# An attention and maxout kernel: weight loads cut in halves and moved among the first value casts, w_out asked for ahead of a cast, and two small swaps of order

## The chip, the cores and the metric

One core of a Trainium2 chip runs the whole program. The metric is the device time of one execution in microseconds (us). Three executions of the kernel before took 290.01 to 290.74 us, median 290.72.

## The reference

Attention over 8 batches and 8 heads, with 576 queries of width 64, whose keys and values are 16 beacon rows followed by 576 causal rows; the result, turned to 4608 tokens of width 512, goes through a feed-forward layer that takes the maximum of three products before the last one.

```python
B, H, S, Nb, D = (8, 8, 576, 16, 64)
k_all = np.concatenate([beacon_k, k], axis=2)
v_all = np.concatenate([beacon_v, v], axis=2)
scores = scale * np.matmul(q, k_all.transpose(0, 1, 3, 2))
scores = np.where(causal, -1000000000.0, scores)      # causal part only for the 576 rows
a = np.exp(scores - scores.max(-1, keepdims=True))
a /= a.sum(-1, keepdims=True) + 1e-09
x = np.matmul(a, v_all).transpose(0, 2, 1, 3).reshape(B * S, H * D)
h = np.maximum(np.maximum(x @ w1, x @ w2), x @ w3)     # w1..w3: 512 x 768
return h @ w_out                                       # w_out: 768 x 512
```

All inputs and the output are float32 in HBM.

## The kernel before

The work goes by pairs of heads: 4 pairs to a batch (`PPB`), 32 in all, two pairs to a quad. For a pair, PE turns q and k so that the width lies on the partitions (L410 for batch 0, L391 later; from batch 4 on, transposing DMAs do it), then computes the scores by tiles of 128 keys. ACT takes the exponential into `at_sb`. GpSimd (POOL) sets the causal part of the diagonal tiles to zero (`affine_select`, L538) or, where `dve` is given, VectorE (DVE) multiplies it with a triangle (L536). PE then multiplies with ones (the sums) and with the values `v_sb` (L582 in batch 0, L615 later), ACT inverts the sums by Ln and Exp, and DVE multiplies (L661 in batch 0, L638 later) into `xT`, the input of the feed-forward layer. That layer runs as units of eight or four matmuls (L720 for the first tokens, L691 later, L739 for the last product with `w_out`), which are slotted in between the attention steps, so that PE always has something to do.

The order is written out by hand; there is no scheduler. Every engine works through its own list in the order of the program, and so do the two issuers of loads: SP (hardware queue q1), which loads q, k, v and the beacons as float32 and stores the output, and POOL (software queue q0), whose DMAs cast to bfloat16 on the way: the quads of q and k for batch 0 (L253), the three input weights (L329, one DMA for each half of 256 rows) and `w_out` (L334). A DMA that POOL issues therefore waits until POOL has done what stands ahead of it.

The steps that the change touches stand in `first_batch` and `second_batch`, in short names. `T` turns a half pair and `S_(p, g)` computes the scores of group g of pair p and their exponential (L483 and L492). `M(p, g)` masks a group; with `True` it does so on DVE, else on POOL. `V(t)` casts value tile t of batch 0 on POOL (L319), after its load on SP has landed. `P(quad, half)` multiplies with ones and values. `invert_sums` and `multiply` make the products L661: for each quad and half three of them, kept in a list from which `multiply(count)` takes the first. `F()` emits the next unit of the feed-forward layer; its first six are the products of the first 256 tokens with weight 1 (three units) and weight 2 (three), each a pair of 128 columns, eight matmuls; the matmuls of a unit read all four row tiles of the weight, that is both halves.

In `second_batch` the masks of a pair of batch 1 alternate with casts on POOL: `cast_piece` and `cast_pair` (L262) for the q and k of pairs further on, `cast_v` (L307) for the values of batch 1. `next_load` takes the next load of batches 2 and on from a list and issues it on SP; the buffers that the loads go to are eight in turn, and a load waits until the cast that read the buffer before has been made. The beacons of batches 4 to 7 come in that same list ahead of the loads of batch 4; POOL casts them at L813.

Of the kernel before, what the change touches and what calls it, by code (L numbers as in the profile page):

```python
# [16 lines left out]
def kernel(  # L17
# [13 lines left out]
    nc = tc.nc  # L31
# [5 lines left out]
    d_model, d_ff = moe_w1.shape  # L37
# [21 lines left out]
    n_quad = 2  # L59
# [108 lines left out]
    w_in = [const.tile([128, n_ct, d_ff], BF16, name=f"w{i}_sb") for i in range(3)]  # L168
# [48 lines left out]
    def load_pair(p, gate=None):  # L217
        b, g, j0 = place(p)
        hs = slice(head(g, j0), head(g, j0) + 2)
        st = new_stage(("pair", p))  # L220
        if gate:
            gate.memset(st[0:QP, 0:1], 0.0)
        for i, src in enumerate((q, k)):
            nc.sync.dma_start(
                out=st[0:QP, i * NQ2 : (i + 1) * NQ2].rearrange("p (h x) -> p h x", h=2),
                in_=src[b, hs].rearrange("h (p r) d -> p h (r d)", r=QR),
            )
# [47 lines left out]
    def load_v(b, piece, gate=None):  # L275
        st = new_stage(("v", b, piece))
        if gate:
            gate.memset(st[:, 0:1], 0.0)
        t_lo, t_hi = V_PIECES[piece]
        for t in range(t_lo, t_hi):  # L280
            i = t - t_lo
            dst = st[:, i * H * D : (i + 1) * H * D].rearrange("p (h d) -> p h d", h=H)
            lo = 0
            if t == 0:
                lo = Nb
                nc.sync.dma_start(
                    out=dst[0:Nb], in_=beacon_v[b].rearrange("h n d -> n h d")
                )
            t0 = k_tok[t] + lo
            n = k_rows[t] - lo  # L290
            nc.sync.dma_start(
                out=dst[lo : lo + n], in_=v[b, :, t0 : t0 + n, :].rearrange("h p d -> p h d")
            )

    def cast_v(b, piece, cast):
        st = stage.pop(("v", b, piece))
        if b not in v_tiles:
            v_tiles[b] = v_pool.tile([128, n_kt, H, D], BF16, name="v_sb")
        v_sb = v_tiles[b]
        t_lo, t_hi = V_PIECES[piece]  # L300
        t = t_lo
        while t < t_hi:
            t1 = t + 1
            while t1 < t_hi and k_rows[t1] == k_rows[t]:
                t1 += 1
            n = k_rows[t]
            cast(  # L307
                v_sb[0:n, t:t1].rearrange("p t h d -> p (t h d)"),
                st[0:n, (t - t_lo) * H * D : (t1 - t_lo) * H * D],
            )  # L310
            t = t1
# [11 lines left out]
        if t + 1 == V_PIECES[piece][1]:  # L323
            stage.pop(("v", 0, piece))

    def load_w(i, f0, f1):
        wv = (moe_w1, moe_w2, moe_w3)[i].rearrange("(g p e) f -> g p e f", g=n_quad, e=2)
        for g in range(n_quad):
            nc.gpsimd.dma_start(  # L329
                out=w_in[i][:, 2 * g : 2 * g + 2, f0:f1], in_=wv[g, :, :, f0:f1]  # L330
            )

    def load_w_out():
        nc.gpsimd.dma_start(  # L334
            out=w_out_sb, in_=moe_w_out.rearrange("(t p) m -> p t m", p=128)
        )
# [60 lines left out]
    def fill(at_bank, n):  # L397
        for _ in range(n):
            nc.tensor.matmul(
                acc[:, at_bank], busy[:, 0:128], busy, start=True, stop=True  # L400
            )
# [242 lines left out]
    def invert_sums():  # L644
        if not unfinished:
            return
        quad, hf = unfinished.pop(0)
        ps = pv_tiles.pop((quad, hf))
        recip = nrm_pool.tile([128, S], FP32, name="recip")[:, 0:HALF]
        nc.scalar.activation(out=recip, in_=ps[0][:, 0:HALF], func=AF.Ln)  # L650
        nc.scalar.activation(out=recip, in_=recip, func=AF.Exp, scale=-1.0)
        for n in range(1, len(passes)):
            products.append((quad, hf, n, ps, recip))

    def multiply(count=len(passes)):
        for _ in range(min(count, len(products))):
            quad, hf, n, ps, recip = products.pop(0)
            b, g = divmod(quad, n_quad)
            c0 = b % RING * S + hf * HALF
            part, bank, lo, ca, cb = passes[n]  # L660
            nc.vector.tensor_mul(  # L661
                xT[:, 2 * g + part - 1, c0 + ca : c0 + cb],
                ps[bank][:, lo : lo + cb - ca],
                recip[:, ca:cb],
            )
            if g == n_quad - 1 and n == len(passes) - 1:
                ready[0] = 2 * b + hf
# [129 lines left out]
    def emit_ffn(limit, new_ps=ffn_psum.tile, close=False):  # L797
        if not may_emit(limit):
            return False
        need, fn, args = units[done[0]]  # L800
        done[0] += 1
        fn(*args, new_ps, *([True] if close else []))
        return True
# [23 lines left out]
    def next_load(n=1):  # L827
        for _ in range(n):
            if loads:
                loads.pop(0)()  # L830
# [45 lines left out]
    S_, T, M, P, V = emit_scores, turn_part, emit_masks, emit_pv, cast_first_v  # L876

    def F(n=1, new_ps=ffn_psum.tile):
        for _ in range(n):
            assert emit_ffn(END, new_ps)  # L880

    def first_batch():
        S_(0, 0)
        T(2, 0, 0, 6)
        S_(1, 0)
        T(2, 0, 1, 7, None, 3)
        T(3, 0, 0, 4)
        T(3, 0, 1, 5)
        V(0)
        V(1)  # L890
        fill(6, 2)
        S_(2, 0)
        M(0, 0, True)
        T(0, 1, 0, 6)
        T(1, 1, 0, 4)
        S_(3, 0)
        M(1, 0, True)
        T(0, 1, 1, 7, None, 2)
        T(1, 1, 1, 5)
        V(2)  # L900
        load_w(0, 0, d_ff)
        S_(0, 1)
        T(2, 1, 0, 6)
        S_(0, 2)
        M(2, 0, True)
        M(0, 1)
        S_(0, 3)
        T(2, 1, 1, 7, None, 2)
        T(3, 1, 0, 6)
        S_(1, 1)  # L910
        M(3, 0, True)
        T(3, 1, 1, 7)
        V(3)
        M(0, 2)
        V(4)
        P(0, 0, 0, 1)
        S_(1, 2)
        M(0, 3, True)
        P(0, 0, 1)
        M(1, 1)  # L920
        invert_sums()
        S_(1, 3)
        P(1, 0, apart=True)
        M(1, 2)
        invert_sums()
        M(1, 3, True)
        load_w(1, 0, d_ff)
        multiply()
        S_(2, 1)
        by_pool(bk16_1, bk32_1)  # L930
        multiply()
        load_pair(PPB, nc.vector)
        for p in range(PPB + 1, 2 * PPB):
            load_pair(p)
        load_v(1, 0)
        load_v(1, 1)
        next_load(2)
        S_(2, 2)
        P(0, 1)
        S_(2, 3)  # L940
        M(2, 1)
        invert_sums()
        F()
        S_(3, 1)
        M(2, 2)
        multiply()
        F()
        S_(3, 2)
        M(2, 3, True)
        F()  # L950
        S_(3, 3)
        M(3, 1)
        M(3, 2)
        M(3, 3, True)
        cast_pair(PPB, by_pool, by_pool)
        next_load()
        P(1, 1)
        invert_sums()
        turn_beacons(1, B_PE, bk16_1)
        F(2)  # L960
        turn_pair(PPB, by_act)
        place_beacons(PPB, by_act)
        cast_pair(PPB + 1, by_pool, by_pool)
        next_load()
        load_w(2, 0, d_ff)
        F()
        multiply()
        free_banks[:] = [2, 3, 0, 1, 6, 7, 4, 5]

    def second_batch():  # L970
        for p in range(PPB, 2 * PPB):
            place_beacons(p + 1, by_act)
            emit_burst(p)
            for gi in range(NG):
                emit_masks(p, gi)
                if p < PPB + 2 and 0 < gi < 3:
                    cast_piece(p + 2, gi - 1, by_pool)
                if p == 2 * PPB - 1 and gi == 1:
                    cast_v(1, 1, by_pool)
                    next_load()  # L980
            if p < PPB + 2:
                stage.pop(("pair", p + 2))
                next_load()
            if p == PPB + 2:
                cast_v(1, 0, by_pool)
                next_load()
                load_w_out()
            if p + 1 < 2 * PPB:
                turn_pair(p + 1, by_dve)
                F(2, next_psum)  # L990
        F(4, next_psum)
        for p in range(2 * PPB, 2 * PPB + 2):
            cast_pair(p, by_pool, by_pool)
            next_load()
        finish = emit_pv_whole(n_quad)
        turn_pair(2 * PPB, by_dve)
        F(2, next_psum)
        finish()
# [94 lines left out]
```

## Time and profile before

| | |
|---|---|
| Runs | 290.01, 290.72, 290.74 us |
| The profiled execution | 289.66 us, span 287.9 us, clock 1.00 |
| PE busy | 276.0 us, 96% of the span |
| DVE, ACT, POOL busy | 173.8, 159.8, 135.7 us |
| DMA | 50.59 MB moved, mean 176 GB/s |
| Chain that ended last, by engine | PE 79%, DMA 12%, POOL 3%, ACT 2%, DVE 1% |
| DMA in that chain | w_out 4%, v 4%, w1 to w3 3%, q 1% |
| Weight 1 to 3, per half | 384 KB, median 7.6 us from issue to landing |
| w_out | 768 KB, 12.4 us from issue to landing |

The span is counted from the program's first instruction to its last; the time of the profiled execution is 1.8 us longer. The chain is followed back from the last instruction to whatever released each step, so its shares tell which work set the end. The timelines give, for each group of instructions of an engine, its start, its length and, in brackets, how long the engine was idle before it and what ended that. In the lists by stretch, a DMA share of 1 means that the 16 DMA engines together were as busy with packets as the stretch is long; packets of two queues that overlap on an engine can bring it above 1.

### The profile page before, as it was taken

To read this page: it belongs to the slowest core of one execution; us is meant where nothing else is said; L and a number is where in the kernel's file an instruction comes from. 1 tells how busy PE (TensorE), PEld (TensorE's weight loads), DVE (VectorE), ACT (ScalarE), POOL (GpSimd) and SP (SyncE) were. 2 spreads that over 40 slices of the span, in tenths; PEclk is the share of its full clock that TensorE was granted. 3 is DMA by queue.
4 is the path that set the end of the run, shared out by engine and by line. 5 is a ranking of instruction groups with operands and counts; after the bars stand their busy time and mean duration, and the time that the engine had idled before them with its cause. 6 is when DMAs were issued, how large, how long until landed. Compare 5 with 4: busy or idle time off the path is not lost.

```text
span 287.9 us, 7656 instructions
## 1 busy us (share of the span) xinstructions
PE 276.0 (96%) x3020; PEld 157.3 (55%) x3020; DVE 173.8 (60%) x303; ACT 159.8 (56%) x299; POOL 135.7 (47%) x281
## 2 busy tenths in 40 slices
PE   7887999989999999999999999999999999999995
PEld 4454765555555555555555787555555554444442
DVE  3784476646583738364846383638464847786773
ACT  3695587685768585766666666756675640000000
POOL 7181788748439692648364835484336210000000
PEclk9999999999999999999999999999999999999999
DMA  7989999999999999979998999995522002003004
GB/s 143 194 157 233 236 219 234 250 214 249 261 232 265 279 248 262 210 174 286 263 214 196 285 286 215 188 232 114 96 75 75 0 2 110 36 3 146 0 0 146
DMA packets 85315, 50.59 MB, mean 176 GB/s; under 512 B 64416, under 2 KB 80032, under 8 KB 85280
## 3 DMA queue, kind: packets, MB, share of 16 engines
q1 hardware_dynamic: 80672, 45.76, 70.0%
q0 software_dynamic: 4048, 4.03, 8.6%
q8 instruction: 23, 0.38, 0.6%
q10 hardware_dynamic: 560, 0.33, 0.5%
q14 instruction: 12, 0.10, 0.1%
HBM read 35.13 MB, written 14.22 MB: 171 GB/s over the span
## 4 chain that ended last, share of the span: by engine, by line
PE 79%; DMA 12%; POOL 3%; ACT 2%; DVE 1%; issue 1%; POOLq 0%; DVEq 0%; ACTq 0%
PE acc L691 43%; PE acc L739 15%; PE acc L615 9%; PE acc L498 7%; DMA w_out_sb<-in_moe_w_out_dram 4%; DMA st<-in_v_dram 4%; PE acc L720 3%; DMA w_sb<-in_moe_w_dram 3%; PE acc L391 2%; POOL v_sb L307 1%; ACT at_sb L516 1%; DMA h<-in_q_dram 1%; POOL p L262 1%; POOL at_sb L538 1%; PE acc L582 0%
## 5 line engine op out<-in xcount | busy, mean ns | idle before, releaser
L691 PE MATMUL acc<-xT,w_sb 128*128 128x512 bf16 (+4 forms) x744 | 135.3, 338 | 0.0
L709 DVE TENSOR_TENSOR hT<-hT,acc 128x512 bf16<-128x512 bf16 x102 | 70.0, 687 | 58.9 <-PE acc L691 54.2
L691 PEld LDWEIGHTS <-w_sb 128*128 128x128 bf16 x744 | 69.2, 98 | 59.6
L538 POOL TENSOR_SCALAR_AFFINE_SELECT at_sb<-at_sb 128x256 bf16<-128x256 bf16 (+2 forms) x176 | 61.8, 371 | 77.6 <-ACT at_sb L516 70.6
L516 ACT ACTIVATE at_sb<-acc 128x208 bf16<-128x208 f32 (+3 forms) x140 | 89.5, 737 | 5.8 <-PE acc L498 4.5
L739 PE MATMUL acc<-w_out_sb,hT 128*128 128x512 bf16 (+2 forms) x246 | 48.4, 348 | 1.3 <-DMA w_out_sb<-in_moe_w_out_dram 1.3
L262 POOL CAST p<-st 96x768 bf16<-96x768 f32 x56 | 44.5, 821 | 2.5 <-DMA st<-in_q_dram 1.8
L746 DVE COPY y<-acc 128x512 f32<-128x512 f32 (+1 forms) x35 | 21.9, 628 | 22.0 <-PE acc L739 16.5
L739 PEld LDWEIGHTS <-hT 128*128 128x128 bf16 x246 | 22.6, 98 | 23.0 <-DVE hT L709 1.6
L711 ACT CAST hT<-acc 128x352 bf16<-128x352 f32 x18 | 8.1, 452 | 47.5 <-PE acc L691 47.5
L711 DVE CAST hT<-acc 128x512 bf16<-128x512 f32 (+1 forms) x48 | 26.6, 554 | 9.6 <-PE acc L691 9.3
L498 PE MATMUL acc<-qT,kT 64*128 64x208 bf16 (+1 forms) x336 | 27.3, 279 | 1.4 <-DVE hT L730 0.6
L764 ACT COPY y<-acc 128x320 f32<-128x320 f32 x1 | 0.4, 425 | 46.0 <-PE acc L757 46.0
L615 PE MATMUL acc<-at_sb,v_sb 128*32 128x512 bf16 (+5 forms) x672 | 23.0, 281 | 0.3 <-POOL v_sb L307 0.3
L498 PEld LDWEIGHTS <-kT 64*128 64x128 bf16 x336 | 15.5, 94 | 14.0 <-issue 3.2
L638 DVE TENSOR_TENSOR xT<-raw,recip 128x576 bf16<-128x576 f32 x28 | 21.7, 816 | 0.1
L615 PEld LDWEIGHTS <-v_sb 128*32 128x32 bf16 (+1 forms) x672 | 14.5, 96 | 7.3 <-POOL v_sb L307 0.7
L307 POOL CAST v_sb<-st 128x1536 bf16<-128x1536 f32 (+2 forms) x21 | 18.3, 893 | 0.0
L625 ACT COPY raw<-acc 128x512 f32<-128x512 f32 x28 | 15.8, 637 | 4.5 <-PE acc L615 4.3
L492 ACT ACTIVATE at_sb<-acc 128x1024 bf16<-128x1024 f32 (+3 forms) x16 | 13.3, 861 | 5.8 <-PE acc L483 5.8
L615 PE MATMUL acc<-at_sb,ones 128*32 128x512 bf16 (+3 forms) x336 | 14.9, 284 | 0.0
L720 PE MATMUL acc<-xT,w_sb 128*128 128x256 bf16 x96 | 12.0, 273 | 1.2 <-DMA w_sb<-in_moe_w_dram 1.2
(68 smaller groups left out, 169.5 us busy)
## 6 DMA issues: line engine op xcount, KB each, us to landing
out_dram<-y SPq DMA_DIRECT2D x35, 256.0 KB, 3.9
st<-in_q_dram SPq DMA_DIRECT2D x28, 288.0 KB, 5.5
st<-in_k_dram SPq DMA_DIRECT2D x28, 288.0 KB, 6.0
st<-in_v_dram SPq DMA_DIRECT2D x24, 256.0 KB, 5.4
w_sb<-in_moe_w_dram POOLq DMA_DIRECT2D x6, 384.0 KB, 7.6
q_dram<-p SPq DMA_DIRECT2D x16, 144.0 KB, 3.4
k_dram<-p SPq DMA_DIRECT2D x16, 144.0 KB, 3.3
st<-in_v_dram SPq DMA_DIRECT2D x8, 224.0 KB, 6.2
```

Of the source, the lines that this page charges most:

```text
L262: cast(t16.rearrange("p r h d -> p h r d"), st[0:QP, i * NQ2 : (i + 1) * NQ2].rearrange("p (h r d) -> p h r d", h=2, r=QR),)
L307: cast(v_sb[0:n, t:t1].rearrange("p t h d -> p (t h d)"), st[0:n, (t - t_lo) * H * D : (t1 - t_lo) * H * D],)
L498: nc.tensor.matmul(ps, kTs[p % NT][hs, 128 * t : 128 * t + 128], qTs[p % NT][hs, q0:q1], start=True, stop=True, tile_position=(64 * e, 0),)
L516: nc.scalar.activation(out=both_heads(p, gi)[:, e0:e1], in_=acc[:, first + e0 : first + e1, 0 : g_width(p, gi)], func=AF.Exp, scale=scale,)
L538: nc.gpsimd.affine_select(out=view, in_=view, compare_op=ALU.is_ge, fill=0.0, base=x0, pattern=[[0, 2], [1, hi - lo]], channel_multiplier=-1,)
L615: nc.tensor.matmul(acc[32 * j : 32 * j + 32, bank, lo + q0 - qa : lo + qb - qa], lhsT, at_view(PPQ * quad + j // 2, t, j % 2, q0, qb), sta ...
L638: nc.vector.tensor_mul(xT[:, 2 * g + i, c0 : c0 + S], raw[:, i], recip)
L691: nc.tensor.matmul(ps[:, a:b], w_in[i][:, ct, 128 * ft : 128 * (ft + 1)], xT[:, ct, x0 : x0 + b - a], start=(ct == 0), stop=(ct == n_ct - 1),)
L709: nc.vector.tensor_max(h[:, lo:hi], h[:, lo:hi], ps[:, lo:hi])
L711: (by_act if hi < TOKB else by_dve)(h[:, lo:hi], ps[:, lo:hi])
L739: nc.tensor.matmul(ps[:, lo:hi], hT[:, ft, 128 * tt : 128 * (tt + 1)], w_out_sb[:, ft, lo:hi], start=(ft == 0), stop=(ft == n_ft - 1),)
L746: (by_act if hi < d_model else by_dve)(y[:, lo:hi], ps[:, lo:hi])
```

## The change

- `load_w` loads any of the two halves of a weight. Weight 1's first half is asked for after `V(1)` and its second after `V(2)`; before, both stood after `V(2)`.
- Weight 2's first half is asked for after `V(3)`, ahead of the POOL masks that follow; its second stands where both stood before.
- The first three products (quad 0) stand ahead of the mask `M(1, 3)` on DVE, not behind it.
- The scores of group 3 of pair 3 come before the third unit of the feed-forward layer, not after it.
- In batch 1, behind the masks of its third pair, `w_out` is asked for before the cast of the first three value tiles, not after it.

The number of instructions on every engine stays the same; weights 1 and 2 are still two DMAs each.

```diff
-    def load_w(i, f0, f1):
+    def load_w(i, gs=range(n_quad)):
         wv = (moe_w1, moe_w2, moe_w3)[i].rearrange("(g p e) f -> g p e f", g=n_quad, e=2)
-        for g in range(n_quad):
-            nc.gpsimd.dma_start(
-                out=w_in[i][:, 2 * g : 2 * g + 2, f0:f1], in_=wv[g, :, :, f0:f1]
-            )
+        for g in gs:
+            nc.gpsimd.dma_start(out=w_in[i][:, 2 * g : 2 * g + 2], in_=wv[g])
...
         V(0)
         V(1)
+        load_w(0, [0])
         fill(6, 2)
         S_(2, 0)
         M(0, 0, True)
...
         V(2)
-        load_w(0, 0, d_ff)
+        load_w(0, [1])
         S_(0, 1)
...
         V(3)
+        load_w(1, [0])
         M(0, 2)
         V(4)
         P(0, 0, 0, 1)
...
         invert_sums()
+        multiply(3)
         M(1, 3, True)
-        load_w(1, 0, d_ff)
-        multiply()
+        load_w(1, [1])
         S_(2, 1)
         by_pool(bk16_1, bk32_1)
         multiply()
...
         F()
         S_(3, 2)
         M(2, 3, True)
+        S_(3, 3)
         F()
-        S_(3, 3)
         M(3, 1)
...
-        load_w(2, 0, d_ff)
+        load_w(2)
...
             if p == PPB + 2:
+                load_w_out()
                 cast_v(1, 0, by_pool)
                 next_load()
-                load_w_out()
```

## Prediction

> **What bounds the kernel now.** I read the chain of work that ended last first, then the timelines of PE, POOL and SP, then the DMA share by stretches. From about 105 us on the chain is PE almost without a gap, so whatever moves the kernel happens before that. Two long DMA pieces stand in the chain of the opening:
>
> ```profile
> 4.16 11.41 DMA st<-in_v_dram
> 15.56 0.05 issue
> 15.62 0.61 POOL v_sb L319
> 16.23 0.51 POOL w_sb L329
> 16.74 7.24 DMA w_sb<-in_moe_w_dram
> ...
> 47.41 12.41 DMA w_out_sb<-in_moe_w_out_dram
> 59.82 0.05 issue
> 59.86 1.47 PE acc L739 x6
> ```
>
> Columns are start, length, what. Weight 1's second half is requested only at 16.74, because POOL works in order and its cast V(2) waits for values that land at 15.56; it lands at 23.98. The timeline of PE shows what that costs (idle time and its releaser in brackets):
>
> ```profile
> 20.56 0.68 PE L582 MATMUL acc<-at_sb,ones 128*32 128x288 bf16 x20 [0.65 <-DVE xT L661]
> 22.40 0.39 PE L720 MATMUL acc<-xT,w_sb 128*128 128x256 bf16 x2
> 24.02 0.83 PE L720 MATMUL acc<-xT,w_sb 128*128 128x256 bf16 x6 [1.23 <-DMA w_sb<-in_moe_w_dram]
> 28.64 0.39 PE L582 MATMUL acc<-at_sb,ones 128*32 128x288 bf16 x8 [0.54 <-DVE at_sb L536]
> 59.86 1.47 PE L739 MATMUL acc<-w_out_sb,hT 128*128 128x512 bf16 x6 [1.28 <-DMA w_out_sb<-in_moe_w_out_dram]
> ```
>
> The change addresses these four idles. What feeds them is DMA, so I looked at how full it is when the request could be made (stretch, clock, busy PE, PEld, DVE, ACT, POOL, clock, then DMA share and GB/s):
>
> ```profile
> 14.00:15.00 1.00, 0.69 (x12) 0.41 (x8) 0.87 (x4) 1.00 (x2) 0.00 (x0) 1.00 1.24 254
> 15.00:16.00 1.00, 1.00 (x18) 0.43 (x17) 0.30 (x2) 0.83 (x2) 0.38 (x1) 1.00 0.66 145
> 16.00:17.00 1.00, 0.89 (x24) 0.63 (x22) 1.00 (x4) 0.76 (x1) 1.00 (x3) 1.00 0.29 60
> 17.00:18.00 1.00, 1.00 (x42) 0.64 (x42) 1.00 (x2) 0.97 (x3) 1.00 (x3) 1.00 0.62 90
> ```
>
> Between 15 and 18 the DMA engines are short of work by 0.34 + 0.71 + 0.38 = 1.43 us; by the same view they are at 0.75 to 1.42 in every microsecond from 18 to 82. This hole is the only new room: everything else the change moves is an exchange of places.
>
> **Weight 1 in halves.** The first half is now issued after V(1), whose cast starts at 13.06 and takes 0.61: at 13.67, not 16.18. The second stays behind V(2), and one issue (0.55, from 1.11 for two) has left the way to it. If V(2) stayed where it is, the second half would be asked for at 16.2. But the first half's packets, about 1 us after the issue as before, meet the tail of the value loads, which are 256-byte packets. How they fare beside weight packets is seen later, where weight 3 passes batch 1's values (DMA queues, 38.5 to 41.5: packets' time as a share of 16 engines):
>
> ```profile
> DMA packets 341, 0.63 MB, mean 209 GB/s; under 512 B 148, under 2 KB 148, under 8 KB 341
> q0 software_dynamic: 210, 0.59, 100.3%
> q1 hardware_dynamic: 131, 0.03, 7.8%
> ```
>
> The values (q1) crawl until the weights are through; just before, from 36 to 37.5, q1 moved 1099 packets. A half is 0.39 MB as written; from 17.5 to 24.5 q0 moved 1.25 MB in 7 us, so a half takes 2.2 us. V(2) is thus delayed by 0 to 2.2; with under 1 us of its load left when the half comes, I take 1.2, in the middle. The Trainium skill (DMA: Bandwidth & Descriptors, Queues, rings and completion order) has each engine alternate between queues by packets of typically 9 to 17 descriptors; by that rule V(2) loses only some 0.5 us (an estimate from that page), the gain worked out below would be 1.5 for 1.1, and case (c) of the rivals would all but fall. The rows speak against it for this mix, 131 small packets to 210 large.
>
> V(2) then is cast from 16.8 to 17.4. Second half: 17.4 + 4.9, the time to landing of the first half in the profile (the second's 7.24 includes waiting for the first) = 22.3. Behind V(2) on POOL stand the second half's issue 0.55, a mask 0.47, V(3) 0.60, weight 2's first half 0.54 (newly ahead of the masks), a mask 0.32, V(4) 0.60, two masks 0.68: the last ends near 21.1, 1.3 later than the 19.79 now. Who waits: P(0,0)'s value products, now at 17.15, wait to 17.4, and P(0,1), which reads these masks, now at 20.56, finishes some 0.3 later. PE so reaches the first weight product at 22.7, the half is there, and eight matmuls (0.98) end at 23.7 against 24.85. Gain **1.1**. With a delay of 2.2: V(2) cast until 18.4, half at 23.3, masks at 22.1, P(0,1) until 23.35, end at 24.6: 0.25. With none: 22.1 + 0.98 = 23.1: 1.8.
>
> **First products ahead of a mask.** Three L661 products (0.28 each) come before one L536 mask (0.60): they end that much sooner, so P(0,1) can start at 20.0 instead of 20.56, but its tile 2 then waits for the mask until 20.7. Net 0.3 at best; hidden under the later masks above, and counted in that bound of 1.8.
>
> **Weight 2 in halves.** It landed at 28.3 and is first read at 30.2. Its second request moves from 20.28 to about 21.0, still ahead of SP's pair loads at 21.52. Cost zero; cover 1.9 us, of which the earlier PE takes 1.1.
>
> **Scores (3,3) before the third product.** The exp can start when that of (3,2) ends at 27.24, not 27.66. But the mask behind it on DVE (L536, at 28.35) has in front of it the L728 copy of the product that is now issued 0.25 later: 27.66 + 0.62 = 28.28. Of the idle 0.54 that leaves 0.07; bounds 0 and 0.54; I take **0.1**.
>
> **w_out before the cast of values.** Its issue (0.85) and the L307 cast (1.41) change places: 1.41 sooner, the cast 0.85 later, with the next mask on POOL where it was (48.27). The cast's reader, the L615 value product at 50.9, needs the end of L307's second group at 50.14, which does not move. If 12.4 us to landing holds, it lands 1.41 sooner against PE, which wants it 1.28 sooner: the whole wait goes. Bounds 0.5 (the engines are full at 1.05 to 1.27 then) and 1.28; I take **1.25**. SP's load behind the cast is not reached until 61.53, so it costs nothing.
>
> **What comes late next.** 1.1 + 0.1 + 1.25 = 2.45, if nothing else holds. Something does (POOL, then PE):
>
> ```profile
> 84.10 0.61 POOL L813 CAST bk<-bk 64x512 bf16<-64x512 f32 x1 [7.42 <-DMA bk<-in_beacon_k_dram]
> 84.67 1.86 POOL L538 TENSOR_SCALAR_AFFINE_SELECT at_sb<-at_sb 128x256 bf16<-128x256 bf16 x6
> 87.02 0.87 PE L615 MATMUL acc<-at_sb,ones 128*32 128x512 bf16 x20
> ```
>
> The masks that P at 87.02 reads end at 86.48 and stand behind a beacon cast that waits for DMA. PE has 0.54 to spare there; beyond that it gains only what the beacon load gains. SP issues almost without a break from 41.8 to 84.9, each load held by an earlier landing, so that load moves by what the DMA engines gained: the hole of 1.43, from 0.5 (part of it lost again in the dips at 44 to 46 and 78 to 83) to 1.43. I take 1.3. The cap is 0.54 + 1.3 = **1.84**, under 2.45. After it, the transposed loads of the later batches land 7 us and more before the scores that read them, so nothing else caps.
>
> Sum: 1.8. The profiled execution took 289.66 (span 287.9); it would take 287.9. It lies 1.06 under the median 290.72 of the runs; from the median the same 1.8 gives **288.9**.
>
> **Rivals.** (a) The beacon load does not move: the hole is filled, but SP's window of loads gives it back. Cap 0.54: 290.2. For it: dips of DMA share to 0.42 to 0.9 at 78 to 83; against: shares over 1 nearly everywhere before. (b) w_out lands when it did, the engines being full: 1.2 remains, 289.5. Against: its request would be first in a queue (q0) with nothing else in it. (c) Slower: the values starve. If V(2) can't finish until the first half has landed altogether (4.0 us after its first packets in the profile, so 18.7, and V(2) at 19.2, cast until 19.8), the second half is requested at 19.8 and, now among the pair loads, takes the 7.24: 27.0. PE waits 3.0 longer than now, w_out gives 1.28 back: 292.4. It decides from a landing of the second half at 25.2 on, where 24.0 is today's and 1.28 is what w_out returns. For it: the 131 packets above; against: only the tail of V(2) is left at 14.6, and one half occupies the engines 2.2 us, not 4. The skill's page (DMA: Bandwidth & Descriptors, Issuing engines are not separate DMA queues) leans this way too: requests of POOL and SP interleave on the same engines, so an earlier one buys no bandwidth. The hole from 15 to 18 is why I don't follow it to the end here.
>
> **Chances.** Forecast 0.66, (a) 0.14, (b) 0.08, (c) 0.12. About 0.3% (0.87 us) is what a measurement of this kernel can tell from no change. (b) is mostly over it, 0.06 of 0.08: faster 0.72, same 0.16, slower 0.12. The range goes from 288.1 (2.6: no delay of V(2), and a cap moved by its full bound and some PE slack) to 290.5 (case (a) and the spread of the runs); it leaves out (c) and some ends.
>
> **What would show it.** Right: the first L329 issue near 13.7; V(2)'s cast between 15.6 and 17.8; no wait of L720 on w_sb over 0.3; PE's wait on w_out under 0.2; the beacon cast L813 at 82.6 to 83.2, and then P's L615 with a small new wait on POOL's masks. Wrong: V(2)'s cast after 18.4, a wait on w_sb as long as before, or L813 still at 84.

## The result: 0.6% faster, as forecast

| | before | after |
|---|---|---|
| Median, lowest and highest of the runs made together | 290.41 (289.22 to 291.38) | 288.80 (287.59 to 289.33) |
| Ratio, 95% interval | | 0.994 (0.9913 to 0.9967) |
| Profiled execution, and its span | 289.66, 287.9 | 287.94, 286.1 |

One execution of the kernel before, run beside e1 to e4, took 975.69 us and is left out of every number here.

The lines named here that stand after `load_w` are two lower: L718 is L720 of before, L737 is L739, L613 is L615, L811 is L813, L580, L534 and L536 are L582, L536 and L538.

The timeline of PE after, at the four idles that the change addresses, with one line ahead of them (start, length, idle before in brackets):

```profile
18.91 0.20 PE L580 MATMUL acc<-at_sb,ones 128*32 128x48 bf16 x2 [0.35 <-DVE at_sb L534]
...
20.32 0.68 PE L580 MATMUL acc<-at_sb,ones 128*32 128x288 bf16 x20
...
22.16 1.05 PE L718 MATMUL acc<-xT,w_sb 128*128 128x256 bf16 x8
...
26.84 0.39 PE L580 MATMUL acc<-at_sb,ones 128*32 128x288 bf16 x8 [0.46 <-DVE at_sb L534]
...
56.72 1.47 PE L737 MATMUL acc<-w_out_sb,hT 128*128 128x512 bf16 x5
```

Three brackets are gone: P(0,1) starts without its 0.65, the eight matmuls of the first weight product run in one piece from 22.16, and the first product with `w_out` waits for nothing. The idle ahead of P(1,1) went from 0.54 to 0.46. One is new: 0.35 inside P(1,0), at 18.91, where two matmuls wait for a mask on DVE. The timeline of POOL shows the first half of weight 1 issued at 13.24. V(2) is 0.41 sooner than before, but so was V(1) in this execution (12.60 for 13.06):

```profile
13.24 0.57 POOL L329 DMA_DIRECT2D w_sb<-in_moe_w_dram  x1
15.21 0.61 POOL L319 CAST v_sb<-st 128x512 bf16<-128x512 f32 x1 [1.40 <-DMA st<-in_v_dram]
15.76 0.55 POOL L329 DMA_DIRECT2D w_sb<-in_moe_w_dram  x1
```

Two of the stretches that held the hole, with the same columns as before (the last three are clock, DMA share, GB/s):

```profile
16.00:17.00 1.00, 0.89 (x26) 0.63 (x22) 1.00 (x3) 0.83 (x1) 0.99 (x3) 1.00 1.04 194
17.00:18.00 1.00, 1.00 (x42) 0.70 (x41) 1.00 (x2) 0.97 (x3) 0.99 (x3) 1.00 1.14 168
```

The shares of 0.29 and 0.62 have become 1.04 and 1.14: the hole is filled. What caps PE later hangs on the beacon cast (timelines of POOL and PE after):

```profile
82.69 0.61 POOL L811 CAST bk<-bk 64x512 bf16<-64x512 f32 x1 [9.15 <-DMA bk<-in_beacon_k_dram]
83.25 1.86 POOL L536 TENSOR_SCALAR_AFFINE_SELECT at_sb<-at_sb 128x256 bf16<-128x256 bf16 x6
85.06 3.13 POOL L262 CAST p<-st 96x768 bf16<-96x768 f32 x4
...
83.88 1.50 PE L613 MATMUL acc<-at_sb,ones 128*32 128x512 bf16 x20
...
88.25 0.43 PE L389 MATMUL acc<-ident,p 96*128 96x96 bf16 x6 [0.19 <-ACT recip L629]
```

The cast is 1.41 sooner. PE is still too early for what stands behind it on POOL: twenty matmuls that wait for the masks and took 0.87 now stretch over 1.50, and the turn of the pair that POOL casts next is split in two halves of six, the second at 88.25, right after the last of those casts ends at 88.19. (The bracket names ACT, which had been done; in the profiles of e2, e5, e6, e7 and e11 the same bracket names POOL's casts.)

To see where time comes and goes I use one quantity throughout: the **lead**, how much earlier PE reaches the same instruction than in the profile of before. After: 1.65 behind the first product, 1.80 ahead of `w_out`, 3.14 behind it, 2.15 behind the beacons, and 1.81 from 182 to the end, which is the gain in the span.

### The profile page after: what moved, and what is told of

The parts are those of the page before. It is cut to its first block, busy times and chain, and to the rows that moved or that the text cites. A ratio compares the mean times of both kernels' runs of the same rounds, so it can differ in the third digit from the quotient of the medians.

```text
span 286.1 us, 7627 instructions
## 1 busy us (share of the span) xinstructions
PE 275.1 (96%) x2990; PEld 157.6 (55%) x3020; DVE 174.5 (61%) x303; ACT 159.4 (56%) x299; POOL 136.9 (48%) x281
## 4 chain that ended last, share of the span: by engine, by line
PE 76%; POOL 5%; issue 1%; DVE 1%; ACT 0%; POOLq 0%
PE acc L689 44%; PE acc L737 14%; PE acc L613 10%; PE acc L496 6%; POOL p L262 2%; POOL at_sb L536 2%; PE acc L389 1%; POOL v_sb L307 1%; PE acc L755 0%; DVE hT L707 0%; DVE qT L423 0%; ACT at_sb L514 0%; DVE y L762 0%; DVE y L744 0%; POOLq L262 0%
## 5 line engine op out<-in xcount | busy, mean ns | idle before, releaser
L536 POOL TENSOR_SCALAR_AFFINE_SELECT at_sb<-at_sb 128x256 bf16<-128x256 bf16 (+2 forms) x176 | 63.1, 379 | 71.1 <-ACT at_sb L514 66.9
L737 PE MATMUL acc<-w_out_sb,hT 128*128 128x512 bf16 (+2 forms) x241 | 48.0, 347 | 0.3
L737 PEld LDWEIGHTS <-hT 128*128 128x128 bf16 x246 | 22.6, 98 | 21.7 <-DVE hT L707 1.6
L613 PE MATMUL acc<-at_sb,v_sb 128*32 128x512 bf16 (+5 forms) x672 | 23.1, 281 | 0.3 <-POOL v_sb L307 0.3
L613 PEld LDWEIGHTS <-v_sb 128*32 128x32 bf16 (+1 forms) x672 | 14.7, 96 | 7.2 <-POOL v_sb L307 0.7
L613 PE MATMUL acc<-at_sb,ones 128*32 128x512 bf16 (+4 forms) x336 | 15.5, 284 | 0.1
L434 DVE COPY kT<-acc 128x576 bf16<-128x576 bf16 x12 | 9.0, 752 | 5.9 <-PE acc L389 5.9
```

Source lines behind the costliest of these rows:

```text
L536: nc.gpsimd.affine_select(out=view, in_=view, compare_op=ALU.is_ge, fill=0.0, base=x0, pattern=[[0, 2], [1, hi - lo]], channel_multiplier=-1,)
L613: nc.tensor.matmul(acc[32 * j : 32 * j + 32, bank, lo + q0 - qa : lo + qb - qa], lhsT, at_view(PPQ * quad + j // 2, t, j % 2, q0, qb), sta ...
L737: nc.tensor.matmul(ps[:, lo:hi], hT[:, ft, 128 * tt : 128 * (tt + 1)], w_out_sb[:, ft, lo:hi], start=(ft == 0), stop=(ft == n_ft - 1),)
```

## The experiments

All ratios are to the kernel before, run on the same chip. The mean granted TensorE clock of an execution was 1.00, or fell to 0.98 to 0.994 where the clock dipped to half early on; 0.998 comes from a drop in the last microsecond too, as in e11's profile. The share of executions with a dip differs between comparisons, so the table also has the median of the full-clock executions alone (mean clock 0.999 or more, their number in brackets) minus that of before in the same comparison: 289.85 for e1 to e4, 289.74 for e5 to e8 and 289.54 for e9 to e12, from 20, 12 and only 4 executions. With the executions at 0.998 counted in, the differences move by 0.2 at most, e11's to -1.3. From the profile of each kernel come the landing of the beacons and three leads.

| kernel | ratio (95%) | full-clock difference | beacons landed | lead ahead of w_out | ahead of 84 | at the end |
|---|---|---|---|---|---|---|
| after | 0.994 (0.9913, 0.9967) | | 82.54 | 1.80 | 3.15 | 1.81 |
| e1 | 0.9989 (0.9955, 1.0022) | -0.2 (8) | 83.64 | -0.79 | -0.51 | -0.52 |
| e2 | 0.9957 (0.9927, 0.9987) | -0.7 (6) | 83.59 | 0.51 | 1.85 | 1.08 |
| e3 | 0.9905 (0.987, 0.994) | -2.1 (7) | 84.71 | 1.25 | 2.59 | 1.97 |
| e4 | 1.0015 (0.9976, 1.0055) | +0.2 (2) | 84.20 | -0.65 | 0.70 | 0.10 |
| e5 | 0.9942 (0.9908, 0.9976) | -1.1 (7) | 82.59 | 1.47 | 2.82 | 1.76 |
| e6 | 0.9987 (0.9962, 1.0011) | -0.2 (7) | 84.99 | 0.08 | 1.20 | -0.64 |
| e7 | 0.9942 (0.9912, 0.9972) | -1.6 (8) | 81.74 | 1.93 | 3.28 | 2.61 |
| e8 | 0.9932 (0.9905, 0.9959) | -2.1 (9) | 82.63 | 0.66 | 2.01 | 1.65 |
| e9 | 0.9930 (0.9902, 0.9959) | -0.9 (11) | 85.33 | -0.08 | 1.27 | 1.25 |
| e10 | 0.9917 (0.9887, 0.9947) | -1.7 (6) | 82.79 | 0.04 | 0.66 | 0.64 |
| e11 | 0.9913 (0.9879, 0.9947) | -1.9 (2) | 84.13 | 1.70 | 3.05 | 0.18 |
| e12 | 0.9968 (0.9935, 1.0) | -0.5 (6) | 74.63 | 0.22 | 1.45 | 1.07 |

My theory was the prediction's: the halves and `w_out` each remove a wait, and the landing of the beacons caps what is kept. Its rivals were that the DMA stream alone decides, or that either part does it all.

### e1: the halves alone

```diff
 # before, with the new load_w
         V(1)
+        load_w(0, [0])
...
         V(2)
-        load_w(0, 0, d_ff)
+        load_w(0, [1])
...
         V(3)
+        load_w(1, [0])
...
-        load_w(1, 0, d_ff)
+        load_w(1, [1])
```

> The kernel before with only the weight 1 and 2 halves moved; w_out, the first products and the scores of (3,3) stay. Theory (the opening gains, and a cap at the beacon cast lies above that gain): the wait of L720 on weight 1 is gone, PE is 1.6 us ahead at the last product of batch 0, the 1.3 us wait on w_out stays or shrinks a little, the beacon cast comes 1.2 to 1.4 sooner than 84.1, and the end is 1.6 us sooner (286.3 span, ratio 0.9945). Rival (the values of batch 0 starve and the hole in DMA only moves): PE's wait turns up at the values instead, under 0.5 us is gained.

A miss: no gain that can be told from none. The loads of this profiled execution came late (V(1) at 13.49, for 13.00 in before's), and two more things stood against it. PE still waits at `w_out`, which is issued when POOL gets to it (48.20, for 47.41 in before's profile) and lands at 60.33; a lead cannot pass that point. And a stall that I had not foreseen stands in the place of the wait on weight 1 (timeline of PE):

```profile
23.09 0.94 PE L718 MATMUL acc<-xT,w_sb 128*128 128x256 bf16 x7
24.30 0.27 PE L718 MATMUL acc<-xT,w_sb 128*128 128x256 bf16 x1 [0.28 <-issue]
...
32.97 0.46 PE L389 MATMUL acc<-ident,p 96*128 96x96 bf16 x7 [0.90 <-issue]
```

"issue" means that the engine waited for nothing that the profile shows. e7 takes this up.

### e2: w_out ahead of the cast, alone

```diff
 # before
             if p == PPB + 2:
+                load_w_out()
                 cast_v(1, 0, by_pool)
                 next_load()
-                load_w_out()
```

> The kernel before with only w_out asked for ahead of the cast of batch 1's values. Theory of the cap: the 1.28 us wait on w_out is gone and PE is 1.3 ahead at 60 us, but the beacons land at 84.0 as before, so that P at 87 waits for its masks and only about 0.5 us arrives at the end (287.4 span, ratio 0.998). Rival (no cap, parts add up): 1.28 us arrives (286.6, ratio 0.9955).

`w_out` lands at 56.75 and PE's lead rises by 1.34 there, the whole of the old wait. Behind the beacons it falls from 1.85 to 1.09, and stays. The cap is there, but at 1.09 and not at 0.5, and the ratio is the one that the rival without a cap had named (0.9957 for 0.9955). The time alone would not have told the two apart; the trace does.

### e3: the changed kernel, the beacon cast one pair later

```diff
-    at_step(B_PE * PPB - 6, 1, L(by_pool, bk16, bk32))
...
-            at_step(p + i - 5, 0, C(cast_pair, p + i, by_pool, by_pool))
+            first = p + i == B_PE * PPB
+            at_step(p + i - 5, 1 if first else 0, C(cast_pair, p + i, by_pool, by_pool))
+            if first:
+                at_step(p + i - 5, 1, L(by_pool, bk16, bk32))
```

> The changed kernel with the cast of the beacons of batches 4 to 7 on POOL moved from ahead of pair 11's masks to behind them, and the cast of pair 16 moved behind that of pair 13 and ahead of the beacons. Theory of the cap: PE keeps its lead of 3.1 us over the kernel before through P at 84 and the turn after it, where the changed kernel falls back to 2.15: another 0.8 to 1.0 us is gained, 285.2 span, ratio to the kernel before 0.991. Rival (DMA as a whole sets the pace there, not the cast's place): the wait turns up at another cast or load within 20 us, and the span stays near 286.1.

The timelines of POOL and PE:

```profile
88.06 0.61 POOL L811 CAST bk<-bk 64x512 bf16<-64x512 f32 x1
...
84.43 0.86 PE L613 MATMUL acc<-at_sb,ones 128*32 128x512 bf16 x20
```

The masks now stand ahead of the cast and end at 81.46, PE's twenty matmuls take 0.86 again, and the lead of 2.59 passes 84 and 88 whole; 0.24 is lost near 100 and 0.37 at 182. This kernel had the lowest ratio of the twelve. In its comparison with before it beats that kernel; against the changed kernel the intervals overlap.

### e4: the halves one cast sooner still

```diff
         V(0)
-        V(1)
         load_w(0, [0])
+        V(1)
+        load_w(0, [1])
...
         V(2)
-        load_w(0, [1])
```

> The changed kernel with weight 1's halves one value cast sooner still: the first after V(0), the second after V(1). Theory (the weight packets queue behind the quads on POOL's queue, so they start near 14.4 whatever the request, and then both halves run on without a break): V(2) lands within 0.4 us of the changed kernel's, V(3) and V(4) land 1 to 2 us later, P(0,1) waits for its masks 0.5 us, weight 1 is there at 19.5, and the time is that of the changed kernel within 0.6 us. Rival (c) of the prediction (values starve beside weight packets): V(2) lands 1.5 to 2.2 us later, PE waits on P(0,0) by as much, and at least 0.9 us is lost against the changed kernel.

Here the values starve, which rival (c) of the prediction had feared, but one tile later than it said. V(2) lands at 15.04 as ever, V(3) at 19.98 for 16.42 (timeline of POOL):

```profile
15.10 0.62 POOL L319 CAST v_sb<-st 128x512 bf16<-128x512 f32 x1 [1.73 <-DMA st<-in_v_dram]
...
20.03 0.61 POOL L319 CAST v_sb<-st 128x512 bf16<-128x512 f32 x1 [3.96 <-DMA st<-in_v_dram]
```

From 16 to 19.5 the queue of the values moved 741 packets in 3.5 us beside 0.54 MB of weight; in the changed kernel from 14 to 17 it was 1217 in 3 us. This execution also had a dip of the clock, from about 15 to 21, so its lead cannot be split between the two. The dip does not explain the late V(3): e6 and e12 had one at the same place, and there V(3) landed at 16.59 and 16.20. As for the time, its two executions at full clock took 289.7 and 290.5 us, 1.4 us above the changed kernel's 288.68 (the median of 11) in the mean. By these two the whole gain is gone.

### e5: the changed kernel again

The same source as after, beside the kernels that follow.

> The changed kernel once more, on the chip of the three that follow. Ratio 0.994 to the kernel before as at first; in the trace PE's lead over the kernel before is 1.2 to 1.8 us after the first product (two earlier executions of this opening differed by 0.6), 1.3 to 1.4 more at the first product with w_out, and falls back to 2.0 to 2.2 behind the beacon cast if it was above that.

The gain and the ledger repeat: 2.82 ahead of the beacons, 2.11 behind them, 1.76 at the end.

### e6: the changed kernel with whole weights

```diff
         V(1)
-        load_w(0, [0])
...
         V(2)
-        load_w(0, [1])
+        load_w(0)
...
         V(3)
-        load_w(1, [0])
...
-        load_w(1, [1])
+        load_w(1)
```

> The changed kernel with weights 1 and 2 asked for as before (both halves after V(2), and after the masks), all other edits kept. Theory now: the halves take away the wait on weight 1, but part of it comes back as PE waiting for its next 256 instructions (0.3 to 0.7 us at the end of the first product in three executions), so the halves are worth 0.5 us: ratio 0.996. The prediction's term: 1.1 us, but with w_out's 1.25 in the sum and the cap at the beacons near 0.9 without the halves' DMA gain, ratio 0.997. Rival (the halves bring nothing): 0.994.

Without the halves 0.85 us of the 1.06 of e5 is gone at full clock (the two intervals of the ratios just overlap). The ratio is 0.9987, where the expectation had 0.996, the prediction's term 0.997 and the rival 0.994. So the halves are probably worth most of the gain within the whole change, while alone (e1) they gave little. The profile points at the way: the hole is back (DMA share 0.46 from 16 to 18, as in before, for 1.14 in e5), the beacons land at 84.99, not 82.59, and the lead falls from 1.20 to -0.30 behind them. Single landings scatter, so the mean says more: 83.2 over the nine profiles with weight 1 in halves and the load of the beacons in its place, 84.5 over the four without (before, e2, e6, e9).

### e7 and e8: twelve instructions fewer ahead

e7 is the changed kernel with fewer but longer filling matmuls at the start, which move every later PE instruction 12 places forward in PE's program; e8 has the same and the beacon cast of e3.

```diff
-        keep_busy(12)
+        keep_busy(8, 480)
...
-        keep_busy(3)
+        keep_busy(2, 480)
...
-        keep_busy(2)
+        keep_busy(1, 512)
```

> The changed kernel with the same columns of filling matmuls on ones at the start cut into fewer, longer ones (8 of 480 for 12 of 320, 2 of 480 for 3 of 320, 1 of 512 for 2 of 320), so that PE's list is 12 instructions shorter ahead of the first score. Theory (PE stalls at every 256th instruction when its next block of 16 KB has not come through the DMA engines): any such stall moves from the end of the first product to 12 instructions later, behind scores (3,1), and is 0.7 us shorter; the stall that one execution had at instruction 959 moves 12 instructions as well. Gain over the changed kernel 0 to 0.5 us. Rival (the stall belongs to the product, not to the count): it stays at the last matmul of the first product.

> The changed kernel with both the later beacon cast and the fewer filling matmuls. Theory: the beacon cast's 0.8 to 1.0 us and up to 0.5 us of the instruction stalls add up, ratio to the kernel before 0.989. Rival (the two gain the same microsecond, another load caps both): 0.9905, as with the later beacon cast alone.

The "issue" stall goes with the count of instructions. In e1 to e3 it stood ahead of the last of the first eight products, and in e6 too, without a bracket (the eight took 1.29 for 1.05); in e8 it stands 12 instructions further on in the work, behind the first of the next eight (timeline of PE):

```profile
24.76 0.93 PE L718 MATMUL acc<-xT,w_sb 128*128 128x256 bf16 x7 [0.30 <-issue]
```

e7 had no stall of that size (its next eight took 1.18 for 1.05), the earliest beacons and the largest lead of all profiles (2.61 at the end); its ratio is that of e5, so the fills are worth nothing that I can tell. e8 reached neither 0.989 nor the rival's 0.9905; at full clock it gained 2.1, as e3 did. Its lead ahead of the beacons was only 2.01, just below where the cap would have stood for its landing (2.06), so its profile says nothing of the cast's place.

### e9: w_out sooner and the beacon cast later, no halves

e2 and the edit of e3 together, on the kernel before.

> The kernel before with w_out ahead of the cast of values and with the beacon cast one pair later (behind pair 11's masks), the weights whole. My theory, that the masks behind the beacon cast cap PE's lead at 0.73 + (83.96 - landing of the beacons), and that nothing else takes it: w_out's 1.28 comes whole and is still there at the end, together with whatever this execution's opening gives, some 0.3 lost later: ratio 0.9955 (0.994 to 0.9975), and PE's lead after P at 84 to 88 as large as before it. Rival, that PE is held at 84 to 88 by something else than those masks (for instance the stretched value products, or the turn behind them): the lead falls there as it did with w_out alone (1.86 to 1.10), and the ratio stays near 0.997. A second rival, that the DMA stream and not PE sets the end: with the stream unmoved the ratio is 0.999 or 1.

This is e2 without the cap. The ratio flatters it, since 15 of the 25 executions of before in this comparison had a mean clock of 0.994 or less and only one of its own 12; at full clock it gained 0.9. In its profile the theory's 1.28 comes out: the wait on weight 1 is still there, the one on `w_out` is gone, and a lead of 1.27 passes 84 and reaches the end as 1.25 (timeline of PE):

```profile
24.07 0.83 PE L720 MATMUL acc<-xT,w_sb 128*128 128x256 bf16 x6 [1.31 <-DMA w_sb<-in_moe_w_dram]
...
58.59 1.47 PE L739 MATMUL acc<-w_out_sb,hT 128*128 128x512 bf16 x6
...
85.75 0.86 PE L615 MATMUL acc<-at_sb,ones 128*32 128x512 bf16 x20
```

Beacons that land at 85.33, the latest of all, cost it nothing. The second rival (the stream sets the end) falls with that.

### e10: without the two swaps of order

```diff
         invert_sums()
-        multiply(3)
         M(1, 3, True)
         load_w(1, [1])
+        multiply()
...
-        S_(3, 3)
         F()
+        S_(3, 3)
```

> The changed kernel with the two swaps of order undone: the first products stand behind the mask again, and the scores (3,3) behind the third feed-forward unit. My theory: both are worth little, since the lead is cut at the beacons to what the DMA stream allows. PE's lead before the beacons is 0.1 to 0.5 smaller than the changed kernel's, the wait ahead of P(1,1) is near 0.54, and the ratio stays 0.994 to 0.9955. Rival, that the swaps are a term of their own (the mask of pair 3 or the products ahead of P(0,1) being on the path): 0.5 us or more is lost, ratio 0.996 or above.

Nothing is lost: the ratio is not above the changed kernel's, and at full clock it gained 1.7 where e5 gained 1.1, though against four executions of before. Without the first swap the idle ahead of P(0,1) is back at 0.64. That alone does not show what the swap is worth: e1 does not have it either and shows no idle there, because it had lost 0.72 one group earlier, at the same new wait inside P(1,0). And the profiles show a price that I had not seen. All nine kernels with the swaps lose 0.35 to 0.37 within one burst of twelve score matmuls at 182; the four without them (e1, e2, e9, e10) lose at most 0.01 there. The timeline of PE, after and then e10:

```profile
181.02 1.25 PE L496 MATMUL acc<-qT,kT 64*128 64x208 bf16 x12
```

```profile
182.53 0.90 PE L496 MATMUL acc<-qT,kT 64*128 64x208 bf16 x12
```

The path can be followed one step back, in the timeline of DVE, after and then e10:

```profile
181.53 0.33 DVE L744 COPY y<-acc 128x160 f32<-128x160 f32 x1 [0.97 <-PE acc L496]
```

```profile
182.69 0.33 DVE L744 COPY y<-acc 128x160 f32<-128x160 f32 x1 [0.62 <-ACT y L744]
```

The ninth matmul of the burst goes on as this copy of an earlier output ends (181.91 for 181.86). In before and the four without the swaps the copy starts 0.16 into the burst, released by a copy on ACT; in all nine with them it starts 0.5 into it, released by one of the score matmuls. The swaps thus make it wait for a later instruction of PE. Why the program's semaphores come out so, and which of the two swaps does it, is not shown. The times point the same way: e6 is e2 with the two swaps, and gained 0.2 at full clock for 0.7, on another chip.

### e11: weight 2 whole

```diff
         V(3)
-        load_w(1, [0])
...
-        load_w(1, [1])
+        load_w(1)
```

> The changed kernel with weight 2 requested whole, where it was before; weight 1 stays in halves. My theory: cost and gain of weight 2's halves are zero, the ratio that of the changed kernel, 0.994 (0.992 to 0.996); weight 2 lands by 28.5 and no product waits for it. Rival, that its first half, ahead of POOL's masks, fills the hole in the DMA share from 15 to 18: then the beacons land 0.5 or more later (83.1 or above, for 82.6) and the ratio is 0.9955 to 0.997.

Weight 2 lands at 26.68 and no product waits for it; the ratio is not above the changed kernel's. Cost and gain of its halves cannot be told from zero, as forecast. Its profiled execution shows the cap at its hardest: the beacons landed at 84.13 and the lead fell from 3.05 to 0.55 (timeline of PE):

```profile
85.87 1.10 PE L613 MATMUL acc<-at_sb,ones 128*32 128x512 bf16 x18 [1.50 <-POOL at_sb L536]
```

It was also the slowest of its six executions, 289.56 us for a median of 288.10. The rival read the later landing rightly and would have taken it for the kernel's; the other five say that it is that of one execution.

### e12: the beacons' load sooner

```diff
     for b in range(2, B):
-        if b == B_PE:
+        loads += load_pairs(b * PPB, (b + 1) * PPB)
+        if b == B_PE - 1:
             loads.append(L(load_beacons, B_PE, B, bk32))
-        loads += load_pairs(b * PPB, (b + 1) * PPB) + load_v_pieces(b)
+        loads += load_v_pieces(b)
```

> The changed kernel with the load of the beacons moved in the list ahead of batch 3's value loads; the place of the cast is unchanged. My theory, that the cap at 84 is the landing of the beacons and nothing else: they land 7 us or more sooner, POOL's wait of 9.15 ahead of their cast is gone, and PE keeps the lead it had (2.5 to 3.1) past 88; some 0.3 is lost at 182. Ratio 0.991 (0.9885 to 0.9935), like the kernel with a later beacon cast. Rival, that POOL then waits as long at the next cast, whose pair's load lands at 84 to 85 in the same stream, ahead of the same masks: the lead is cut at a later pair (91 to 100) by the same 0.7 and the ratio stays near 0.994.

The mechanism holds, the time does not. The beacons are there at 74.63, POOL casts them without a wait, and the lead of 1.45 passes 84 and 88 uncut. But the lead was small to begin with, because the granted clock fell to half in the opening (timeline of POOL, then a stretch of the trace, in which the third number from the end is the clock):

```profile
75.19 0.61 POOL L811 CAST bk<-bk 64x512 bf16<-64x512 f32 x1
```

```profile
18.00:20.00 2.00, 2.00 (x50) 1.17 (x46) 0.99 (x3) 1.62 (x4) 1.34 (x4) 0.50 1.06 202
```

Its six executions at full clock gained only 0.5 us, less than those of e5. Why they did not gain 2 like e3 stays open: the one profile, with a lead of 1.45, cannot show what would have happened to a lead of 3 at the pair casts behind.

## Why the prediction was right, point by point

**The cap.** The prediction's cap stood at the masks behind the beacon cast: 0.54 of PE's spare time plus what the beacons gain. The place was one step short. PE's products wait there, but they recover part of it; the cut that lasts is at the turn behind, which needs the four pair casts that POOL makes after those masks. Before's own timelines of POOL and PE had it:

```profile
86.48 3.13 POOL L262 CAST p<-st 96x768 bf16<-96x768 f32 x4
...
90.15 0.68 PE L391 MATMUL acc<-ident,p 96*128 96x96 bf16 x12
```

The casts end at 89.61, and the second six of these twelve come at 90.38 by the trace: 0.77 to spare, 0.72 with the 0.05 that the hand-over takes after the cast in the other timelines. Every profile that was cut fits one line, lead behind = 0.73 + (83.96 - landing), where 83.96 is the landing in before:

| kernel | landing | by the line | lead ahead | lead behind P | lead behind the turn |
|---|---|---|---|---|---|
| after | 82.54 | 2.15 | 3.15 | 2.51 | 2.15 |
| e5 | 82.59 | 2.10 | 2.82 | 2.47 | 2.11 |
| e7 | 81.74 | 2.95 | 3.28 | 3.28 | 2.95 |
| e2 | 83.59 | 1.10 | 1.85 | 1.46 | 1.09 |
| e11 | 84.13 | 0.56 | 3.05 | 0.92 | 0.55 |
| e4 | 84.20 | 0.49 | 0.70 | 0.70 | 0.48 |
| e6 | 84.99 | -0.30 | 1.20 | 0.06 | -0.30 |

The two whose lead was below the line, e1 and e10, passed uncut, and so did the four that took the cast or the load out of the way (e3, e8, e9, e12). Of these e3 and e9 are the test: for their landings the line gives -0.02 and -0.64, and they kept 2.59 and 1.27. By the column behind P the masks alone would leave 1.09 + (83.96 - landing), twice my 0.54: the products begin as the first masks are there. The other half of the term was near: the beacons gained 1.42 for the 1.3 that I took. That this is the hole's 1.43 almost to the hundredth is chance, since single landings scatter by more; the means above differ by 1.3. So the cap was 2.15, not 1.84.

**The sum.** It came out at 1.8 in the span because 0.35 was lost at 182, where the prediction had said that nothing else caps. The mechanism was right, a cap below the sum of the parts; that the total agrees to the tenth is luck, two errors that cancel.

**V(2) and the first half.** I took a delay of 1.2. There was hardly any: V(2) landed 2.60 after V(1), before it was 2.56; over the nine profiles with the first half behind V(1) it is 2.73 in the mean (2.4 to 3.0), over the four without 2.62 (2.3 to 3.1). The Trainium skill (DMA: Bandwidth & Descriptors, Queues, rings and completion order), whose alternation by packets made this delay small, was nearer here than the rows I set against it; in e4, with two halves queued, my rows were nearer, V(3) coming 4.9 after V(2) for 1.3. The second half landed at 21.15, not 22.3, the masks ended at 19.39, not 21.1, and the first eight products at 23.21, not 23.7: a gain of 1.64 on the 24.85 of before, for 1.1 taken, near the 1.8 of the bound without delay. Of this 0.24 was there ahead of the product; the rest came where the wait on weight 1 had been. In the six profiles with nearly this opening and no dip (after, e3, e5, e7, e8, e11) the lead behind the product is 0.9 to 2.2, in the mean 1.55.

**First products ahead of the mask.** I netted at most 0.3. The idle of 0.65 ahead of P(0,1) went whole, and the lead rose by 0.73 there. But 0.55 had been lost just before, at the new wait inside P(1,0), behind three masks on DVE that took 2.39 for 1.85 before; from P(1,0) to the first product the lead rose by 0.17 only. In e7 and e11, where these masks took 1.53 and 1.66, nothing was lost there, and the lead rose by 0.66 and 0.79. What makes the masks longer is not shown. By the ratio of e10 the two swaps together are worth nothing at the end.

**Weight 2.** Zero, by e11.

**Scores (3,3).** The idle ahead of P(1,1) went from 0.54 to 0.46: 0.08, for the 0.1 taken. The 0.35 lost at 182 goes with the two swaps and was not foreseen.

**w_out.** Issued at 44.21 and landed 10.7 us later, for 12.4 in before; the wait went whole, 1.28 by the old bracket and 1.34 by the lead, for 1.25 taken. In e9 it went whole to the end.

**Rivals.** (a), the beacon load does not move: false, 1.42. (b), `w_out` lands as before: false, though not by a wide margin, since in e10 and e6 PE still waited 0.66 and 0.17 for it. (c), the values starve: false here, true one cast sooner (e4), which is how near the change stands to the edge. As far as e5 against e6 and the mean landings tell, that the hole is filled is also what the halves are mostly worth at the end: the removed wait on weight 1 lies above the cap, and part of it can go to a block of instructions (below).

## What to carry to other kernels

A wait removed early is worth what the latest of the later caps lets through: list the transfers that PE will meet next, in order, and ask of each whether the change moves its landing too. Filling a hole in the DMA stream can be worth more than the wait that one meant to remove, since the loads behind it in an unbroken stream come sooner: here the beacons by 1.3 us in the mean, for a hole of 1.43. And a forecast that agrees in its total should still be taken apart in a ledger of leads, because two wrong terms can cancel.

## What the runs showed of the hardware that I had not expected

**PE's program seems to come by the same DMA engines.** The list of DMA queues of the changed kernel has:

```profile
q8 instruction: 23, 0.38, 0.6%
```

23 packets of 16 KB for some 6040 matmuls and weight loads, one for every 260 or so; the two stalls of e1 stand 256 of them apart. I read this as PE's program, fetched block by block. The stalls called "issue" stood at such a place (e1, e2, e3, e6, e8): the packet ended 1.3 to 1.6 us before PE went on (in e1 at 22.95 and 31.50, for 24.30 and 32.97), and the packet took 0.9 to 1.3 us. Stalls of 0.25 to 0.9 us came where the packet started late. Around the first product it started 2.5 to 3.5 us after PE had passed the place 256 instructions before in e8, e6, e1, e3 and e2; in e7 and e10, at 2.4 and 2.5, PE lost 0.13 and 0.05 there, and in the changed kernel, e12, e11 and e5, at 1.2 to 2.2, nothing. In before the same packet came 3.7 after, while PE waited for weight 1 anyway. That the late packet causes the stall is read from these times and from the shift in e8; no run changed the packets themselves.

**The opening differs from one execution to the next.** V(1) landed between 11.8 and 13.5 us with nothing changed ahead of its load, and the beacons of kernels with nearly the same opening (after, e5, e7, e10, e11) between 81.7 and 84.1. One profile is thus no measure of a term of half a microsecond.

**The clock.** In 42 of 92 executions of before the mean granted clock was 0.994 or less; their median is 291.4, that of the others 289.8, and the 14 at 0.998 are no slower than these (289.8). In the profiles of e4, e6 and e12 the dip shows as a granted clock of 0.50 for 3 to 7 us from about 15 on. e10 shows another loss, in which the granted clock reads 1.00 while matmuls take longer until 11 (timeline of PE; six matmuls of this form take 0.40 otherwise, and three of the filling ones 0.82):

```profile
7.84 0.61 PE L481 MATMUL acc<-qT,kT 64*128 64x288 bf16 x6
...
9.30 1.46 PE L397 MATMUL acc<-busy 128*128 128x512 bf16 x3
```

A stretch without a record of the clock reads as 1.00 in these views: the trace's first record of the full clock comes at 11.0 in e10, at 4.3 to 7.3 in the others. The late start cost e10's profiled execution 1.2 us of lead by 10.7, and is why its span (287.3) says less for it than its median. The Trainium skill (TensorE: Matmul & The Clock Gate, Part 1: The HAM clock gate) has the array start at half rate and go to full rate after a busy window of about 3.4 us. In the other profiles full rate came 2.8 to 5.8 us after the first matmul at 1.52, which is of that order; e10's does not agree, with PE busy all the time from 1.52 and the full rate 9.5 us later.
